# The second product of an MLP: its stationary operands moved by 16 bytes and read in steps of 1, 2 or 4 words

## The chip, the cores and the metric

The kernel runs on one core of one Trainium2 chip. The metric is the device time of one execution in microseconds (us), smaller is better. A core has five engines with queues of their own: TensorE (PE, matmuls; its weight loads are shown as PEld), VectorE (DVE), ScalarE (ACT), GpSimd (POOL) and SyncE (SP, which issues DMAs here).

## What is computed

Two layers, each of linear attention and an MLP, both with a layer norm in front and added to x. S = 2048 rows, D = 448, F = 1792, 16 heads of 28, all float32.

```python
def _B_ref(x, w1, b1, w2, b2):
    h = jnp.einsum("bsd,df->bsf", x, w1) + b1
    h = _gelu(h)
    return jnp.einsum("bsf,fd->bsd", h, w2) + b2
...
x = A_x
x = x + _A_ref(_layernorm(x, axis=-1), A_wqkv, A_wo)
x = x + _B_ref(_layernorm(x, axis=-1), B_w1, B_b1, B_w2, B_b2)
x = x + _A_ref(_layernorm(x, axis=-1), A_wqkv, A_wo)
x = x + _B_ref(_layernorm(x, axis=-1), B_w1, B_b1, B_w2, B_b2)
```

`_A_ref` is the linear attention: it forms q, k and v, applies phi to q and k, sums k times v over all rows, and divides.

## The kernel before

The 2048 rows are 16 tiles of 128 rows, and 4 tiles make a block. Every float32 product is made of three matmuls on operands in a shorter float format (F32R): each operand is split into a high part (the value rounded to F32R) and a low part (the remainder), and hi x hi, hi x lo and lo x hi are added up in the same PSUM bank.

A layer has a first phase (`phase1`) that runs over the 16 tiles and forms q, k and the sum over all rows, then a short stretch written out by hand as the string `ORDER`, then the MLP over four blocks. The layer's second half of attention for block b + 1 is worked in beside the MLP of block b, by the lists `PLAN_0`, `PLAN_1` and `PLAN`, whose tokens `behind` (lines 948 to 980) turns into calls. The order of all instructions is the order in which the program issues them; each engine works its queue from the front.

The MLP's loop is at lines 1029 to 1063. For each block it runs over i, the NF = 14 chunks of 128 of F. `mlp1` (lines 852 to 869) makes chunk i of the first product for the block's 512 rows: 11 matmuls at lines 858 to 862 with pieces of w1 as weights (the stationary operand, 128 x 128) and the block's x as the moving operand (512 columns), into `hp`. Then ACT applies gelu with the bias (line 864) to give `g`, ACT copies it to `gh` in F32R (line 867), and DVE subtracts to get `gl` (line 868). `gh` and `gl` have 128 partitions (the 128 rows of F of this chunk) and 512 words (the block's 512 rows of x, 128 for each tile j), in two buffers each, tags "A" and "B". `mlp2` (lines 871 to 898) is the second product: for each of the 4 tiles j it takes 128 columns of `gh` or `gl` as weights and a row of w2 (448 columns) as the moving operand, three matmuls at lines 891 to 893, accumulated over i in the PSUM bank `acc[j]`. In the very last chunk of the program the last tile is done in two halves of 224 columns (lines 883 to 885). After chunk 13 DVE adds the bank to x (line 896).

`mlp1` of chunk i + 1 is issued ahead of `mlp2` of chunk i, so that gelu, the copy and the subtraction of a chunk run beside the matmuls of the chunk before. The tags "A" and "B" also hold the split of x in the first phase (lines 442 and 443) and other tiles at lines 689, 776 and 777.

Two smaller places are touched. In layer 0, tiles 0 to 7 are transposed by PE, and the last 64 columns of a tile are copied twice over into a tile `tail` of 128 columns, two buffers (lines 411 to 413). And `b2b` (line 186) is a constant tile of 448 words that a DMA fills with b2 (line 1003), behind the first phase of layer 0; POOL adds it to x at line 820, in chunks 9 to 12 of each block.

Of the kernel before, what the change touches and what calls it, by code (L numbers as in the profile page):

```python
# [9 lines left out]
F32 = mybir.dt.float32  # L10
F32R = mybir.dt.float32r
# [11 lines left out]
def linear_attn_mlp_kernel(  # L23
# [12 lines left out]
    pe, act, dve, pool, sp = nc.tensor, nc.scalar, nc.vector, nc.gpsimd, nc.sync  # L36
# [15 lines left out]
    work = ctx.enter_context(tc.tile_pool(name="work", bufs=2))  # L52
# [9 lines left out]
    def bank(tag, bufs, name):  # L62
        return psum.tile([128, 512], F32, name=name, tag=tag, bufs=bufs)
# [4 lines left out]
        bufs = NH if tag == "H" else bufs  # L68
        return work.tile([128, D], dt, name=name, tag=tag, bufs=bufs)

    def t512(tag, bufs, name, dt=F32):
        return work.tile([128, 512], dt, name=name, tag=tag, bufs=bufs)

    def f(ap):
        return ap.bitcast(F32)
# [82 lines left out]

    ones = consts.tile([128, 128], F32R, name="ones")
    one = t512("e", 3, "one")[:, :128]  # L160
    dve.memset(one, 1.0)
    dve.tensor_copy(ones, one)
# [23 lines left out]
    b2b = consts.tile([128, D], F32, name="b2b")  # L186
# [5 lines left out]
    w2h = wts.tile([128, NF, D], F32R, name="w2h")  # L192
    w2l = wts.tile([128, NF, D], F32R, name="w2l")
# [23 lines left out]
    def ln_norm(stats, name):  # L217
        xs, mv, rs = stats
        xn = t512("xn", 2, name)
        dve.tensor_scalar(xn[:, :D], xs, mv[:, 0:1], rs, op0=OP.subtract, op1=OP.mult)  # L220
        return xn
# [69 lines left out]
    def turn(x, key, t):  # L291
        x = x[:, :D]
        if (key, t // 2) not in squares:
            squares[key, t // 2] = half("sq")
        sq = squares[key, t // 2].rearrange("p (m c u n) -> p c m u n", m=4, c=4, n=32)[:, :, :, t % 2]
        dve.transpose(sq[:, :3], x[:, :TL].rearrange("p (c m n) -> p c m n", c=3, n=32))
        dve.transpose(sq[:, 3].rearrange("p (u m) n -> p u m n", u=2),
                      x[:, TL:].rearrange("p (m n) -> p m n", n=32)[:, None].to_broadcast([128, 2, 2, 32]))
# [34 lines left out]
    def phi(o, name, into=None, tag="e"):  # L333

        e = t512(tag, 3 if tag == "e" else 2, name)[:, :D]
        act.activation(e, o, AF.Relu, scale=-1.0)
        act.activation(e, e, AF.Exp, scale=-1.0)
        into = e if into is None else into
        dve.scalar_tensor_tensor(into, o, 0.0, e, op0=OP.max, op1=OP.add)
        return into  # L340
# [60 lines left out]
    tails = {}  # L401
# [4 lines left out]
    def stage_n(l, t):  # L406

        xs, mv, rs = sts.pop((l, t))
        dve.tensor_scalar(xs, xs, mv[:, 0:1], rs, op0=OP.subtract, op1=OP.mult)
        xns[l, t] = xs  # L410
        if t < TURNED[l]:
            d = tails[l, t] = work.tile([128, 128], F32, name="tail", tag="tail", bufs=2)
            act.copy(d.rearrange("p (u n) -> p u n", u=2), xs[:, None, TL:].to_broadcast([128, 2, 64]))

    def stage_t(l, t):
# [191 lines left out]
    def phase1(l, tr):  # L607
# [6 lines left out]
        for t in range(l == 0, NT):  # L614
            norm = NORM[l][t] if t < len(NORM[l]) else ()
            for tok in STEPS.get((l, t), STEP).split():
                if tok[1:].isdigit() and tok[0] in "anv":
                    {"a": stage_a, "n": stage_n, "v": stage_t}[tok[0]](l, int(tok[1:]))
                elif tok == "q1":
                    stage_qphi(1)  # L620
# [9 lines left out]
                elif tok == "n":  # L630
                    for u in norm:
                        stage_n(l, u)
# [193 lines left out]
    def m_split(l, b, j):  # L826

        if j < 2:
            split_t(("m", l, b), j, *block(("m", l, b)).pieces(j), dve if j else pool)
        else:  # L830
            split_x(("m", l, b), j)
# [18 lines left out]
    gs = {}  # L850

    def mlp1(l, b, i):
        hp = bank("h", 2, "hp")
        s = slice(i * 128, (i + 1) * 128)
        x = blocks["m", l, b]
        o = hp.rearrange("p (t n) -> p t n", t=4)
        for c in range(3):
            pe.matmul(o, w1h[:, c, s], x.moving(x.hi, c), start=(c == 0), stop=False)  # L858
            pe.matmul(o, w1l[:, c, s], x.moving(x.hi, c), start=False, stop=False)  # L859
            pe.matmul(o, w1h[:, c, s], x.moving(x.lo, c), start=False, stop=False)  # L860
        pe.matmul(o, w1x[:, s], x.moving(x.hi, 3), start=False, stop=False)  # L861
        pe.matmul(o, w1x[:, s], x.moving(x.lo, 3), start=False, stop=True)  # L862
        g = t512("e", 3, "g")
        act.activation(g, hp, AF.Gelu_apprx_tanh, bias=b1s[:, i:i + 1])  # L864
        gh = t512("A", 2, "gh", F32R)
        gl = t512("B", 2, "gl", F32R)
        act.copy(gh, g)  # L867
        dve.tensor_sub(gl, g, f(gh))  # L868
        gs[i] = (gh, gl)

    def mlp2(l, b, i, acc):
        gh, gl = gs.pop(i)
        first, last = i == 0, i == NF - 1
        end = l == LAYERS - 1 and b == NB - 1
        for j in range(4):
            t = b * 4 + j
            s = slice(j * 128, (j + 1) * 128)
            if end and j == 3 and last:

                for h, eng in enumerate((act, sp)):  # L880
                    n = slice(h * D // 2, (h + 1) * D // 2)
                    o = bank("m", 2, "yh")[:, :D // 2]
                    pe.matmul(o, gh[:, s], w2h[:, i, n], start=True, stop=False)
                    pe.matmul(o, gh[:, s], w2l[:, i, n], start=False, stop=False)
                    pe.matmul(o, gl[:, s], w2h[:, i, n], start=False, stop=True)
                    xs = xt[l, t][:, n]
                    dve.tensor_tensor(xs, o, xs, op=OP.add)
                    eng.dma_start(x_d[l + 1][t * 128:(t + 1) * 128, n], xs)
                continue
            stop = last or (end and j == 3 and i == NF - 2)  # L890
            pe.matmul(acc[j], gh[:, s], w2h[:, i], start=first, stop=False)  # L891
            pe.matmul(acc[j], gh[:, s], w2l[:, i], start=False, stop=False)  # L892
            pe.matmul(acc[j], gl[:, s], w2h[:, i], start=False, stop=stop)  # L893
            if stop:
                xs = xt.pop((l, t)) if last else xt[l, t]
                dve.tensor_tensor(xs, acc[j], xs, op=OP.add)
                if last:
                    sp.dma_start(x_d[l + 1][t * 128:(t + 1) * 128, :], xs)
# [94 lines left out]
    for l in range(LAYERS):  # L993
        tr = SimpleNamespace(mp={})
        za, acc = phase1(l, tr)
# [9 lines left out]
        def pre(j):  # L1005
# [13 lines left out]
            x=lambda j: m_split(l, 0, j), tu=lambda j: turn(xns.pop(("m", l, j)), ("m", l, 0), j),  # L1019
            st=lambda j: store_sq(("m", l, 0), 0), sp=lambda j: spread(("m", l, 0), 0), pre=pre, b=biases)  # L1020
        for tok in ORDER.split():
            name, j = tok.rstrip("0123456789"), int("0" + tok.lstrip("abcdefghijklmnopqrstuvwxyzQTG"))
            getattr(tok_, name)(j)
        assert not fill and not qo
        table(AF.Gelu_apprx_tanh)
        q_z(l, 1, 0, tr)
        mlp1(l, 0, 0)
        trans_chunks(tr)
        for b in range(NB):
            acc = [bank("acc", 4, f"y{j}")[:, :D] for j in range(4)]  # L1030
# [5 lines left out]
            for i in range(NF):  # L1036
                if i + 1 < NF:
                    mlp1(l, b, i + 1)
                elif nxt:
                    mlp1(l, b + 1, 0)  # L1040
                if l == 0 and b == 0 and i:
                    background(1, 1)
                if i == NF - 2 and not nxt and l + 1 < LAYERS:
                    table(AF.Exp)
                if 9 <= i < 13:
                    add_bias(l, b, i - 9)
                if nxt:
                    behind(l, b, i, tr)
                elif l + 1 < LAYERS:
                    if i == 2:  # L1050
                        split_kq("k", st_k)
                    if i == 5:
                        split_kq("q", st_q)
                    if i in (3, 4, 6, 7, 8):
                        t = (3, 4, 6, 7, 8).index(i)
                        stage_a(l + 1, t)
                        stage_n(l + 1, t)
                        stage_t(l + 1, t)
                        if t % 2:
                            stage_sp(l + 1, t)  # L1060
                    if 9 <= i < 13:
                        stage_x(l + 1, i - 9)
                mlp2(l, b, i, acc)
# [28 lines left out]
```

## Time and profile before

| | |
|---|---|
| median of 2 runs | 877.35 us (877.15 to 877.54) |
| profiled execution, first to last instruction | 875.2 us |
| between that span and the median | 2.1 us |
| mean granted clock of TensorE | 0.999 |
| PE busy | 870.1 us, 99% |
| DVE busy | 491.2 us, 56% |
| ACT busy | 344.4 us, 39% |
| POOL busy | 221.1 us, 25% |

The profile is of one execution. A row of a group reads: line, engine, operation, what is written <- what is read, shapes, count | busy us, mean ns of one | idle time of the engine before it, with what ended most of it. In the timeline the columns are start and length in us, then engine and instruction. Matmuls are pipelined and their ends are modelled, so the length of a matmul is not what it costs in a stream; the distance of two starts is. PEld rows are the weight loads, which overlap matmuls. The blocks of the MLP of layer 0 start at about 143, 221, 299 and 377 us, those of layer 1 at about 573, 656, 734 and 812 us.

### The profile page before, as it was taken

To read this page: it belongs to the slowest core of one execution; us is meant where nothing else is said; L and a number is where in the kernel's file an instruction comes from. 1 tells how busy PE (TensorE), PEld (TensorE's weight loads), DVE (VectorE), ACT (ScalarE), POOL (GpSimd) and SP (SyncE) were. 2 spreads that over 40 slices of the span, in tenths; PEclk is the share of its full clock that TensorE was granted. 3 is DMA by queue.
4 is the path that set the end of the run, shared out by engine and by line. 5 is a ranking of instruction groups with operands and counts; after the bars stand their busy time and mean duration, and the time that the engine had idled before them with its cause. 6 is when DMAs were issued, how large, how long until landed. Compare 5 with 4: busy or idle time off the path is not lost.

```text
span 875.2 us, 11679 instructions
## 1 busy us (share of the span) xinstructions
PE 870.1 (99%) x4182; PEld 772.0 (88%) x4182; DVE 491.2 (56%) x958; ACT 344.4 (39%) x606; POOL 221.1 (25%) x250
## 2 busy tenths in 40 slices
PE   9999999999999999999999999999999999999998
PEld 8999988888888888888899998888888888888887
DVE  7878586658455443226477876864674483433112
ACT  6776635324323322333356665332233133223221
POOL 5566532235013112012222344110220140140000
PEclk9999999999999999999999999999999999999999
DMA  5474637633313402051145543352332423111001
GB/s 160 136 239 152 207 88 210 184 93 125 133 60 105 156 0 97 1 179 49 48 141 188 166 128 106 104 182 80 110 109 91 134 71 115 49 49 43 0 1 43
DMA packets 63642, 94.76 MB, mean 108 GB/s; under 512 B 8928, under 2 KB 58720, under 8 KB 63584
## 3 DMA queue, kind: packets, MB, share of 16 engines
q1 hardware_dynamic: 63408, 93.87, 33.5%
q8 instruction: 33, 0.54, 0.3%
q14 instruction: 25, 0.20, 0.1%
q10 hardware_dynamic: 176, 0.14, 0.0%
HBM read 56.17 MB, written 34.60 MB: 104 GB/s over the span
## 4 chain that ended last, share of the span: by engine, by line
PE 98%; DVE 0%; DMA 0%; POOL 0%; issue 0%; DVEq 0%; POOLq 0%
PE y L893 10%; PE y L892 10%; PE y L891 10%; PE hp L859 9%; PE hp L860 9%; PE hp L858 9%; PE hp L861 3%; PE hp L862 3%; PE psk L326 2%; PE psq L325 2%; PE psq L327 2%; PE psq L326 2%; PE psk L327 2%; PE psk L325 2%; PE G L534 2%; PE G L535 2%
## 5 line engine op out<-in xcount | busy, mean ns | idle before, releaser
L868 DVE TENSOR_TENSOR gl<-g,gh 128x512 fp32r<-128x512 f32 x112 | 82.6, 737 | 300.0 <-ACT gh L867 300.0
L864 ACT ACTIVATE g<-hp,b1s 128x512 f32<-128x512 f32 x112 | 77.1, 688 | 406.6 <-PE hp L862 401.8
L893 PE MATMUL y<-w2h,gl 128*128 128x448 f32 x447 | 163.3, 365 | 0.0
L892 PE MATMUL y<-w2l,gh 128*128 128x448 f32 x447 | 163.3, 365 | 0.0
L891 PE MATMUL y<-w2h,gh 128*128 128x448 f32 x447 | 163.3, 365 | 0.0
L859 PE MATMUL hp<-XH,w1l 128*128 128x512 f32 x336 | 131.5, 392 | 0.0
L858 PE MATMUL hp<-XH,w1h 128*128 128x512 f32 x336 | 131.2, 391 | 0.0
L860 PE MATMUL hp<-XL,w1h 128*128 128x512 f32 x336 | 131.2, 391 | 0.0
L214 POOL TENSOR_TENSOR brs<-bve,mhalf 128x1 f32<-128x1 f32 x64 | 39.4, 616 | 283.9 <-DVE bve L212 280.8
L891 PEld LDWEIGHTS y<-w2h,gh 128*128 128x128 f32 x447 | 84.0, 188 | 9.0
L892 PEld LDWEIGHTS y<-w2l,gh 128*128 128x128 f32 x447 | 84.0, 188 | 8.3
L893 PEld LDWEIGHTS y<-w2h,gl 128*128 128x128 f32 x447 | 84.0, 188 | 6.6
L860 PEld LDWEIGHTS hp<-XL,w1h 128*128 128x128 f32 x336 | 63.1, 188 | 14.1 <-issue 0.6
L859 PEld LDWEIGHTS hp<-XH,w1l 128*128 128x128 f32 x336 | 63.1, 188 | 11.3
L858 PEld LDWEIGHTS hp<-XH,w1h 128*128 128x128 f32 x336 | 63.1, 188 | 10.8
L867 ACT CAST gh<-g 128x512 fp32r<-128x512 f32 x112 | 69.7, 622 | 3.6
L751 POOL TENSOR_TENSOR pz<-pq,zb 128x448 f32<-128x448 f32 x32 | 36.6, 1147 | 82.6 <-DVE dn L757 65.9
L445 POOL TENSOR_TENSOR xnl<-x,xnh 128x384 fp32r<-128x384 f32 x32 | 35.0, 1092 | 72.6 <-ACT xnh L444 40.6
L315 DVE TENSOR_TENSOR XL<-sp,XH 128x512 fp32r<-128x512 f32 x50 | 44.4, 893 | 4.1 <-ACT XH L314 4.1
L862 PE MATMUL hp<-XL,w1x 128*128 128x512 f32 x112 | 43.6, 389 | 0.0
L861 PE MATMUL hp<-XH,w1x 128*128 128x512 f32 x112 | 43.6, 389 | 0.0
L820 POOL TENSOR_TENSOR x<-x,b2b 128x448 f32<-128x448 f32 x32 | 42.0, 1332 | 0.0
(169 smaller groups left out, 1566.8 us busy)
## 6 DMA issues: line engine op xcount, KB each, us to landing
x<-in_A_x_dram SPq DMA_DIRECT2D x32, 224.0 KB, 3.9
pq_d<-eq SPq DMA_DIRECT2D x32, 224.0 KB, 2.8
pq<-pq_d SPq DMA_DIRECT2D x32, 224.0 KB, 3.2
sq_m<-sq SPq DMA_DIRECT2D x14, 512.0 KB, 2.8
sp<-sq_m SPq DMA_DIRECT2D x56, 128.0 KB, 2.9
x<-x_d SPq DMA_DIRECT2D x32, 224.0 KB, 3.2
sq_a<-sq SPq DMA_DIRECT2D x12, 512.0 KB, 2.9
sp<-sq_a SPq DMA_DIRECT2D x48, 128.0 KB, 2.9
```

The source lines that it names most:

```text
L315: eng.tensor_tensor(lo.rearrange("p (c i n) -> p c i n", c=4, n=32), x, f(h), op=OP.subtract)
L858: pe.matmul(o, w1h[:, c, s], x.moving(x.hi, c), start=(c == 0), stop=False)
L859: pe.matmul(o, w1l[:, c, s], x.moving(x.hi, c), start=False, stop=False)
L860: pe.matmul(o, w1h[:, c, s], x.moving(x.lo, c), start=False, stop=False)
L861: pe.matmul(o, w1x[:, s], x.moving(x.hi, 3), start=False, stop=False)
L862: pe.matmul(o, w1x[:, s], x.moving(x.lo, 3), start=False, stop=True)
L864: act.activation(g, hp, AF.Gelu_apprx_tanh, bias=b1s[:, i:i + 1])
L867: act.copy(gh, g)
L868: dve.tensor_sub(gl, g, f(gh))
L891: pe.matmul(acc[j], gh[:, s], w2h[:, i], start=first, stop=False)
L892: pe.matmul(acc[j], gh[:, s], w2l[:, i], start=False, stop=False)
L893: pe.matmul(acc[j], gl[:, s], w2h[:, i], start=False, stop=stop)
```

## The change

`gh` and `gl` get tiles of 576 words, and a chunk's 512 words begin at an offset that depends on the chunk: `gh` at `at(i)`, `gl` at `at(i + 7)`. Most blocks take `i % 16 * 4` words, that is 16 bytes more from chunk to chunk. Inside the 512 words, the columns of the four tiles j are interleaved by a step of 1, 2 or 4 words, which the table `DEALT` gives by layer and block: with 1 they stand as before, each tile's 128 words on end; with 2, two tiles share 256 words, every other word each; with 4, all four share the 512 words, every fourth word each. ACT and DVE write `gh` and `gl` in that order, and PE reads its weights in that step.

| layer, block | step in words | offset of chunk i in words |
|---|---|---|
| 0, 0 | 1 | 4 (i mod 16) |
| 0, 1 | 2 | 4 (i mod 16) |
| 0, 2 | 4 | 4 (i mod 16) |
| 0, 3 | 1 | 8 (i mod 8) |
| 1, 0 | 2 | 4 (i mod 16) |
| 1, 1 | 1 | 4 (i mod 16) |
| 1, 2 | 1 | 4 ((i + 2) mod 16) |
| 1, 3 | 1 | 0 |

All other tiles with the tags "A" and "B" keep offset 0. `tail` has no tile of its own any more; it takes one of two halves of `b2b` in turn.

```diff
-    def t512(tag, bufs, name, dt=F32):
-        return work.tile([128, 512], dt, name=name, tag=tag, bufs=bufs)
+    def t512(tag, bufs, name, dt=F32, at=0):
+        n = 576 if tag in "AB" else 512
+        return work.tile([128, n], dt, name=name, tag=tag, bufs=bufs)[:, at:at + 512]
...
-            d = tails[l, t] = work.tile([128, 128], F32, name="tail", tag="tail", bufs=2)
+            d = tails[l, t] = b2b[:, t % 2 * 128:][:, :128]
             act.copy(d.rearrange("p (u n) -> p u n", u=2), xs[:, None, TL:].to_broadcast([128, 2, 64]))
...
-        gh = t512("A", 2, "gh", F32R)
-        gl = t512("B", 2, "gl", F32R)
-        act.copy(gh, g)
-        dve.tensor_sub(gl, g, f(gh))
-        gs[i] = (gh, gl)
+        step, at = DEALT[l][b]
+        gh = t512("A", 2, "gh", F32R, at(i))
+        gl = t512("B", 2, "gl", F32R, at(i + 7))
+
+        def dealt(x):
+            return x.rearrange("p (h n u) -> p h u n", h=4 // step, u=step)
+
+        g4 = g.rearrange("p (h u n) -> p h u n", h=4 // step, u=step)
+        act.copy(dealt(gh), g4)
+        dve.tensor_sub(dealt(gl), g4, f(dealt(gh)))
+        gs[i] = [dealt(x) for x in (gh, gl)]
+
+    DEALT = (
+        ((1, lambda i: i % 16 * 4), (2, lambda i: i % 16 * 4), (4, lambda i: i % 16 * 4), (1, lambda i: i % 8 * 8)),
+        ((2, lambda i: i % 16 * 4), (1, lambda i: i % 16 * 4), (1, lambda i: (i + 2) % 16 * 4), (1, lambda i: 0)),
+    )
...
-            s = slice(j * 128, (j + 1) * 128)
+            s = (slice(None), j // step, j % step)
...
-            pe.matmul(acc[j], gh[:, s], w2h[:, i], start=first, stop=False)
-            pe.matmul(acc[j], gh[:, s], w2l[:, i], start=False, stop=False)
-            pe.matmul(acc[j], gl[:, s], w2h[:, i], start=False, stop=stop)
+            pe.matmul(acc[j], gh[s], w2h[:, i], start=first, stop=False)
+            pe.matmul(acc[j], gh[s], w2l[:, i], start=False, stop=False)
+            pe.matmul(acc[j], gl[s], w2h[:, i], start=False, stop=stop)
```

The two halves of the last tile (lines 883 to 885) change in the same way.

More of the change, by code (lines that the diff above doesn't have):

```diff
@@ L864, in mlp1 @@
         act.activation(g, hp, AF.Gelu_apprx_tanh, bias=b1s[:, i:i + 1])
-        gh = t512("A", 2, "gh", F32R)
-        gl = t512("B", 2, "gl", F32R)
-        act.copy(gh, g)
-        dve.tensor_sub(gl, g, f(gh))
-        gs[i] = (gh, gl)
+        step, at = DEALT[l][b]
[11 more added lines that the diff above has]
+    )
     def mlp2(l, b, i, acc):
         gh, gl = gs.pop(i)
+        step = DEALT[l][b][0]
         first, last = i == 0, i == NF - 1
@@ L882, in mlp2 @@
                     o = bank("m", 2, "yh")[:, :D // 2]
-                    pe.matmul(o, gh[:, s], w2h[:, i, n], start=True, stop=False)
-                    pe.matmul(o, gh[:, s], w2l[:, i, n], start=False, stop=False)
-                    pe.matmul(o, gl[:, s], w2h[:, i, n], start=False, stop=True)
+                    pe.matmul(o, gh[s], w2h[:, i, n], start=True, stop=False)
+                    pe.matmul(o, gh[s], w2l[:, i, n], start=False, stop=False)
+                    pe.matmul(o, gl[s], w2h[:, i, n], start=False, stop=True)
                     xs = xt[l, t][:, n]
```

## Prediction

> **What bounds the kernel now.** I read the head of the page first, then the waits of PE, then the costliest groups with their shapes kept apart, and last the timeline of one chunk of the MLP.
>
> ```profile
> span 875.2 us, 11679 instructions
> PE 870.1 (99%) x4182; PEld 772.0 (88%) x4182; DVE 491.2 (56%) x958; ACT 344.4 (39%) x606; POOL 221.1 (25%) x250
> PEclk9999999999999999999999999999999999999999
> PE 98%; DVE 0%; DMA 0%; POOL 0%; issue 0%; DVEq 0%; POOLq 0%
> ```
>
> PE has work for the whole span, at a full clock, and 98% of the chain that ended last is PE itself. The waits of PE hold nothing of the MLP:
>
> ```profile
> engine line waited for: us in total, times, longest us
> PE warm L167 <- DVE one L161: 1.1, 1, 1.1
> PE tp L264 <- ACT tail L413: 0.2, 1, 0.2
> ```
>
> So the time changes only where the change makes PE's own instructions longer or shorter, or makes PE wait for gh or gl. What it touches on PE are the three lines of the second product:
>
> ```profile
> L893 PE MATMUL y<-w2h,gl 128*128 128x448 f32 x447 | 163.3, 365 | 0.0
> L892 PE MATMUL y<-w2l,gh 128*128 128x448 f32 x447 | 163.3, 365 | 0.0
> L891 PE MATMUL y<-w2h,gh 128*128 128x448 f32 x447 | 163.3, 365 | 0.0
> ...
> L326 PE MATMUL psq<-wq,XH 128*128 128x448 f32 x96 | 35.1, 366 | 0.0
> ...
> L535 PE MATMUL G<-kl,xnh 128*128 128x448 f32 x90 | 32.9, 365 | 0.0
> ...
> L891 PEld LDWEIGHTS y<-w2h,gh 128*128 128x128 f32 x447 | 84.0, 188 | 9.0
> ```
>
> 3 x 447 = 1341 matmuls. The 365 ns are a modelled length and overlap with the next one's; what counts is start to start. One chunk of layer 0, block 2, in the timeline (start, length, engine):
>
> ```profile
> 299.35 0.36 PE L891 MATMUL y<-w2h,gh 128*128 128x448 f32 x1
> 299.36 0.19 PEld L892 LDWEIGHTS y<-w2l,gh 128*128 128x128 f32 x1
> 299.55 0.37 PE L892 MATMUL y<-w2l,gh 128*128 128x448 f32 x1
> ...
> 301.58 0.37 PE L893 MATMUL y<-w2h,gl 128*128 128x448 f32 x1
> 301.79 0.39 PE L858 MATMUL hp<-XH,w1h 128*128 128x512 f32 x1
> ...
> 304.07 0.39 PE L862 MATMUL hp<-XL,w1x 128*128 128x512 f32 x1
> 304.07 0.19 PEld L891 LDWEIGHTS y<-w2h,gh 128*128 128x128 f32 x1
> 304.29 0.36 PE L891 MATMUL y<-w2h,gh 128*128 128x448 f32 x1
> ```
>
> The 12 matmuls of the second product start from 299.35 to 301.58: 11 gaps, 2.23 us, **203 ns** each. The 11 of the first product start from 301.79 to 304.07: 10 gaps, **228 ns** each. The 64 columns more cost 25 ns, 0.39 ns a column; 448 columns would be 177 ns by that, and 26 ns stand beside them. Each weight load starts within 0.01 us of the start of the matmul before its own. Whether it or the stream of columns sets the 203 ns is seen at the end of the kernel, where only 224 columns stream:
>
> ```profile
> 870.83 0.19 PEld L884 LDWEIGHTS yh<-w2l,gh 128*128 128x128 f32 x1
> 870.93 0.27 PE L884 MATMUL yh<-w2l,gh 128*128 128x224 f32 x1
> 870.94 0.19 PEld L885 LDWEIGHTS yh<-w2h,gl 128*128 128x128 f32 x1
> 871.05 0.27 PE L885 MATMUL yh<-w2h,gl 128*128 128x224 f32 x1
> ...
> 871.38 0.27 PE L885 MATMUL yh<-w2h,gl 128*128 128x224 f32 x1
> ```
>
> With half the columns, and the same weights, the gap falls to (871.38 - 870.93) / 4 = **113 ns**, and a matmul starts 0.10 to 0.11 us after its load started, though the load's row says 0.19 (its tail overlaps). So a contiguous load of 128 columns needs at most 113 ns between matmuls, and the 448 columns hide it with 203 - 113 = 90 ns to spare. That margin decides this case.
>
> **The change part by part.**
>
> *Places 16 bytes further (all blocks but layer 1, block 3).* No instruction is added. A load of 512 bytes a partition begins elsewhere. At worst it touches one more piece of memory, and 90 ns of margin lie over it: I take 0. From below: if the 26 ns beside the columns came from where the weights lie against w2, up to 26 ns could be won in 1341 - 168 = 1173 matmuls (12 x 14 = 168 stay in the block without an offset), 30 us. But psq and G, with other tiles in other places, have the same 366 and 365 ns, so I take no gain and keep that end for a rival. With the margin gone, the offset would cost what the longer load does, below.
>
> *Steps of 2 words (layer 0 block 1 and layer 1 block 0: 336 matmuls).* A load now reaches over 128 x 8 = 1024 bytes a partition instead of 512. The trace shows no load in steps. Ends: 113 ns, if only elements count (hidden), and 2 x 113 = 226 ns, if bytes passed over count at the load's own contiguous rate. The nearest row of a faster reader is the first product's moving operand: 512 x 4 = 2048 bytes a partition in 228 ns, so PE's reading of 1024 bytes fits in 114 ns. I take 114: hidden, cost 0.
>
> *Steps of 4 words (layer 0 block 2: 168 matmuls).* A load reaches over 128 x 16 = 2048 bytes. Ends: 113 ns (hidden, 0) and 4 x 113 = 452 ns. The nearest row is again 2048 bytes of moving operand in 228 ns; twice the load's own 105 ns plus the 10 ns until it starts is 220 ns. I take **220 ns**, which is over the 203: the load ends last, and each gap grows by 17 ns. In a chunk 11 of the 12 loads stand behind a matmul of 448 columns; the first stands behind one of 512, whose 228 ns still hide it. So 14 x 11 = 154 gaps x 17 ns = **2.6 us**.
>
> [...]
>
> *Writing gh and gl in steps (ACT L867, DVE L868).* Same instructions and elements, other places. The chain of one chunk, and of the tightest chunk in a block with steps (layer 1, block 0, chunk 0):
>
> ```profile
> 300.27 0.62 ACT L867 CAST gh<-g 128x512 fp32r<-128x512 f32 x1
> 300.93 0.69 DVE L868 TENSOR_TENSOR gl<-g,gh 128x512 fp32r<-128x512 f32 x1 [2.12 <-ACT gh L867]
> 304.50 0.19 PEld L893 LDWEIGHTS y<-w2h,gl 128*128 128x128 f32 x1
> ...
> 572.01 0.69 DVE L868 TENSOR_TENSOR gl<-g,gh 128x512 fp32r<-128x512 f32 x1 [2.18 <-ACT gh L867]
> 573.14 0.19 PEld L893 LDWEIGHTS y<-w2h,gl 128*128 128x128 f32 x1
> ```
>
> gl is ready at 301.62 and first loaded at 304.50: 2.88 us. Ends: nothing, or both instructions doubled, 0.62 + 0.69 = 1.31 us, still hidden. At 572.70 the reserve is 0.44 us: doubled, PE would wait 0.87 us, once. Behind a longer gl on DVE stand the next block's steps, and DVE is busy only 28.3 of 78 us there (windows):
>
> ```profile
> core 0: us, PE busy (x) PEld busy (x) DVE busy (x) ACT busy (x) POOL busy (x), PEclk, DMA share, GB/s
> 299.00:377.00 78.00, 78.00 (x367) 68.64 (x366) 28.32 (x54) 22.70 (x36) 7.69 (x8) 1.00 0.15 51
> ```
> ```profile
> L315 DVE TENSOR_TENSOR XL<-sp,XH 128x512 fp32r<-128x512 f32 x4 | 2.7, 683 | 0.0
> ```
>
> L315, which reads and writes in another order in runs of 32 words, takes 683 ns beside 691 for gl; that is the nearest row, so I take 0.
>
> *Tail in halves of b2b, larger A and B.* Two halves taken in turn stand where two buffers stood; the eight copies and their transposes are over long before b2b is loaded:
>
> ```profile
> L413 ACT COPY tail<-x x8: 289/298/299, 6.6 to 41.1; 128x128 f32<-128x128 f32 x8
> L257 PE MATMUL tp<-ident,tail x6: 272/272/273, 17.8 to 51.4; 128*128 128x128 f32 x6
> L1003 SPq DMA_DIRECT2D b2b<-in_B_b_dram x1: 1588/1588/1588, 112.3 to 112.3; - x1
> ```
>
> The load on SP's queue gains a wait for the last transpose (51.4 us), 61 us before it is issued; nothing queued behind it moves. If the halves were held as one tile, a copy (0.30 us) could wait for one transpose: at most 8 x 0.3 = 2.4 us; I take 0.
>
> *Sum.* The profiled span is 875.2 us, the median of the runs 877.35, so 2.1 us lie outside it. 875.2 + 0 + 0 + 2.6 + 0 + 0 + 2.1 = 879.9, **880.0 us**.
>
> **The rivals.**
>
> *A. The steps are hidden too.* If the load counts elements alone, it stays at 113 ns under 203, and the time is 877.4. For it: 90 ns of margin. Against it: no row shows a stepped read.
>
> *B. The load takes its reads from the stream.* The 26 ns beside the columns would be the load's reads, and grow with the bytes it reaches over. That is +26 ns in 336 matmuls (8.7 us) and +78 ns in 168 (13.1 us): 21.8 us, 899. With half of the 26 ns, 10.9 us, 888; I put it at 890. For it: 26 ns is much for a mere change of weights. Against it: the trace shows no pair of matmuls without a load to compare. [...]
>
> *C. The load passes over bytes at its own rate.* 226 ns for steps of 2, 452 ns for steps of 4. Then 28 x 11 = 308 gaps x 23 ns = 7.1 us, and in block 2 of layer 0 154 x (452 - 203) = 38.3 us and 14 x (452 - 228) = 3.1 us: 48.5 us, 925.9, slower by 5.5%. It decides by itself, with steps of 4 alone, from a load of x ns with 154 (x - 203) + 14 (x - 228) = 17.5 us, which is 2%: x = 309 ns. For it: 113 ns is the only rate of loading that the trace shows. Against it: PE's other operand passes the same bytes in 228.
>
> *D. Faster.* The 26 ns come from a clash of places and fall away in 1173 matmuls: down to 847; half of it 862. Against it: equal times for all tiles of 448 columns.
>
> *E. A late gl.* The writes double and the tail waits: 880.0 + 0.9 + 2.4 = 883.3.
>
> **How the numbers follow.** My forecast 0.34; A 0.24; B 0.16; C 0.15; E 0.06; D 0.05. The likeliest alone, with a load of 210 to 230 ns, adds 1.1 to 4.2 us: 878.4 to 881.5. For the range I leave out C and D, 0.20 together: from 876.0, just under A, to 899.0, the upper end of B. About 2% is what a measurement of this kernel can tell from no change; that is 859.8 to 894.9. Over it lie C and the upper quarter of B, 0.19; under it most of D, 0.04; within it 0.77.
>
> **What would show it.** In the timeline of layer 0, block 2, second product: 220 ns from start to start (203: A; 240 to 280: B; 300 and more: C), with the load rows there longer than 188 ns. In the blocks with steps of 2: 203 (A and mine), 216 or more (B, C). In blocks with offsets alone 203; less would be D. L867 and L868 by block show what writing in steps costs, and the waits of PE must stay without L891 and L893. I am wrong if the blocks with offsets alone differ from layer 1, block 3, or if the sum of blocks 1 and 2 doesn't give the difference of the spans.

## The result, and the profile after

The changed kernel takes 884.26 us (883.89 to 884.64, 2 runs) against 877.35 us (877.15 to 877.54, 2 runs): 1.0075 times as long, 95% interval 1.0046 to 1.0104. That is 6.9 us more; the forecast was 2.7 us more, in a range of 876.0 to 899.0. The direction is as forecast, the size two and a half times as large. The profiled execution has a span of 882.2 us, 7.0 us more than before. The page's head, its chain, and the costliest groups that changed (lines 904 to 906 are the old 891 to 893, line 874 the old 867, line 875 the old 868):

```profile
span 882.2 us, 11679 instructions
PE 875.9 (99%) x4182; PEld 781.5 (89%) x4182; DVE 496.7 (56%) x958; ACT 351.5 (40%) x606; POOL 221.3 (25%) x250
PE 98%; DMA 1%; DVE 0%; ACT 0%; POOL 0%; issue 0%; SPq 0%; DVEq 0%; ACTq 0%
L875 DVE TENSOR_TENSOR gl<-g,gh 128x512 fp32r<-128x512 f32 x112 | 88.0, 786 | 303.0 <-ACT gh L874 299.2
L906 PE MATMUL y<-w2h,gl 128*128 128x448 f32 x447 | 165.1, 369 | 0.0
L906 PEld LDWEIGHTS y<-w2h,gl 128*128 128x128 f32 x447 | 92.8, 208 | 5.3
L874 ACT CAST gh<-g 128x512 fp32r<-128x512 f32 x112 | 77.7, 694 | 3.6
```

PE is still 98% of the chain, and its waits still hold nothing of the MLP:

```profile
engine line waited for: us in total, times, longest us
PE warm L168 <- DVE one L162: 1.1, 1, 1.1
PE tp L265 <- DVE x L410: 0.7, 1, 0.7
PE tp L265 <- ACT b2b L414: 0.7, 1, 0.7
```

So PE's own instructions became longer. The mean over 447 weight loads of L906, 208 ns instead of 188, hides where. Block by block, the distance from one block's first matmul of the second product to the next block's tells it (starts taken from the trace; the fourth column reaches over the first phase of layer 1, the last one from the first such matmul of layer 1, block 3 to the last):

```
us               start   0,0    0,1    0,2    0,3     1,0    1,1    1,2    1,3
before          143.11  78.12  78.12  78.12  195.47  78.12  78.12  78.12  63.33
after           143.35  78.24  78.48  83.44  195.82  78.42  78.21  78.28  63.33
difference       +0.24  +0.12  +0.36  +5.32   +0.35  +0.30  +0.09  +0.16   0.00
```

They add up to 6.9 us. Of it 5.3 us lie in the one block with steps of 4, 0.7 us in the two blocks with steps of 2, 0.7 us in the four with offsets alone, and 0.2 us in the start. The timeline of the block with steps of 4, to be laid beside the chunk that the prediction shows:

```profile
299.85 0.40 PE L863 MATMUL hp<-XL,w1x 128*128 128x512 f32 x1
300.08 0.37 PE L904 MATMUL y<-w2h,gh 128*128 128x448 f32 x1
300.29 0.40 PE L905 MATMUL y<-w2l,gh 128*128 128x448 f32 x1
300.30 0.33 PEld L906 LDWEIGHTS y<-w2h,gl 128*128 128x128 f32 x1
300.52 0.39 PE L906 MATMUL y<-w2h,gl 128*128 128x448 f32 x1
300.53 0.33 PEld L904 LDWEIGHTS y<-w2h,gh 128*128 128x128 f32 x1
300.75 0.40 PE L904 MATMUL y<-w2h,gh 128*128 128x448 f32 x1
...
302.64 0.40 PE L906 MATMUL y<-w2h,gl 128*128 128x448 f32 x1
302.65 0.21 PEld L859 LDWEIGHTS hp<-XH,w1h 128*128 128x128 f32 x1
302.87 0.39 PE L859 MATMUL hp<-XH,w1h 128*128 128x512 f32 x1
```

The load is 0.33 us long instead of 0.19, and from 300.29 to 302.64 ten gaps take 2.35 us: **235 ns** from start to start, where 203 stood and 220 was forecast. The first gap is 210 ns, and the gap behind the 512 columns of L863 is 230 ns, as before. The gap from the last of the twelve to the first product (302.64 to 302.87) has some 235 ns again, though the load in it is a contiguous one. So eleven gaps of a chunk grow, as counted in the prediction, but in the records each stands one place later than its load; the run on the price of a load shows why.

### The profile page after: what moved, and what is told of

Read it like the earlier page. It is cut to its first block, busy times and chain, and to the rows that moved or that the text cites. A ratio compares the mean times of both kernels' runs of the same rounds, so it can differ in the third digit from the quotient of the medians.

```text
span 882.2 us, 11679 instructions
## 1 busy us (share of the span) xinstructions
PE 875.9 (99%) x4182; PEld 781.5 (89%) x4182; DVE 496.7 (56%) x958; ACT 351.5 (40%) x606; POOL 221.3 (25%) x250
## 4 chain that ended last, share of the span: by engine, by line
PE 98%; DMA 1%; DVE 0%; ACT 0%; POOL 0%; issue 0%; SPq 0%; DVEq 0%; ACTq 0%
PE y L905 10%; PE y L906 10%; PE y L904 10%; PE hp L860 9%; PE hp L861 9%; PE hp L859 9%; PE hp L863 3%; PE hp L862 3%; PE psk L327 2%; PE psq L326 2%; PE psq L327 2%; PE psq L328 2%; PE psk L328 2%; PE psk L326 2%; PE G L537 2%; PE G L535 2%
## 5 line engine op out<-in xcount | busy, mean ns | idle before, releaser
L875 DVE TENSOR_TENSOR gl<-g,gh 128x512 fp32r<-128x512 f32 x112 | 88.0, 786 | 303.0 <-ACT gh L874 299.2
L905 PE MATMUL y<-w2l,gh 128*128 128x448 f32 x447 | 165.2, 370 | 0.0
L906 PE MATMUL y<-w2h,gl 128*128 128x448 f32 x447 | 165.1, 369 | 0.0
L904 PEld LDWEIGHTS y<-w2h,gh 128*128 128x128 f32 x447 | 92.5, 207 | 7.7
L905 PEld LDWEIGHTS y<-w2l,gh 128*128 128x128 f32 x447 | 92.6, 207 | 7.2
L906 PEld LDWEIGHTS y<-w2h,gl 128*128 128x128 f32 x447 | 92.8, 208 | 5.3
L874 ACT CAST gh<-g 128x512 fp32r<-128x512 f32 x112 | 77.7, 694 | 3.6
L863 PE MATMUL hp<-XL,w1x 128*128 128x512 f32 x112 | 43.9, 392 | 0.0
```

Of the source, the lines that this page charges most:

```text
L874: act.copy(dealt(gh), g4)
L875: dve.tensor_sub(dealt(gl), g4, f(dealt(gh)))
L904: pe.matmul(acc[j], gh[s], w2h[:, i], start=first, stop=False)
L905: pe.matmul(acc[j], gh[s], w2l[:, i], start=False, stop=False)
L906: pe.matmul(acc[j], gl[s], w2h[:, i], start=False, stop=stop)
```

## The experiments

Theory 1: a weight load in steps takes longer and, where it outlasts the columns that stream meanwhile, ends last; the offsets act separately, by where weights and moving operand stand to each other. The rivals: B of the prediction, the load takes reads from the stream, so that a step adds the same at every width; that steps of 2 cost by themselves and offsets nothing; that the slower writes hold PE up.

**Steps alone.** All offsets of the changed kernel are 0.

```diff
-        ((1, lambda i: i % 16 * 4), (2, lambda i: i % 16 * 4), (4, lambda i: i % 16 * 4), (1, lambda i: i % 8 * 8)),
-        ((2, lambda i: i % 16 * 4), (1, lambda i: i % 16 * 4), (1, lambda i: (i + 2) % 16 * 4), (1, lambda i: 0)),
+        ((1, lambda i: 0), (2, lambda i: 0), (4, lambda i: 0), (1, lambda i: 0)),
+        ((2, lambda i: 0), (1, lambda i: 0), (1, lambda i: 0), (1, lambda i: 0)),
```

> The changed kernel with every offset set to 0; the steps of 1, 2 and 4 words stay. Theory 1 (the stepped load ends last; the offsets act for themselves by where weights and moving operand stand to each other): layer 0 block 2 keeps its 83.4 us (78.1 before), the blocks with steps of 2 and of 1 go back to 78.1 us, 12 matmuls of the second product to 2.433 us; span 880.4 to 880.8. Rival (steps of 2 cost by themselves, offsets nothing): the two blocks with steps of 2 keep 78.4 to 78.5, the others are at 78.1; span 881.1.

Measured: 883.74 us, ratio 1.0074 (1.0059 to 1.0089), span 881.3. By blocks, in the manner of the table: 78.12, 78.47, 83.86, 195.59, 78.46, 78.12, 78.12, 63.33. The rival is right for steps of 2: they cost 0.35 us a block with no offset at all, half of it in the second product (12 matmuls 2.444 us instead of 2.433) and half in the first product between them (229.4 ns a matmul instead of 228.3). Theory 1 had them free. The blocks with steps of 1 are at 78.12 as both said. The block with steps of 4 costs 5.7 us, so the offsets took 0.4 us off it.

**Offsets alone.** All steps of the changed kernel are 1.

```diff
+        ((1, lambda i: i % 16 * 4), (1, lambda i: i % 16 * 4), (1, lambda i: i % 16 * 4), (1, lambda i: i % 8 * 8)),
+        ((1, lambda i: i % 16 * 4), (1, lambda i: i % 16 * 4), (1, lambda i: (i + 2) % 16 * 4), (1, lambda i: 0)),
```

> The changed kernel with every step set to 1; the offsets stay. Theory 1: layer 0 block 2 falls from 83.4 us to 78.2, the blocks with offsets keep 0.1 to 0.35 us over 78.1, since the time of 12 matmuls depends on the place (2.400 to 2.460 us); span 876.0 to 876.8. Rival (steps cost, offsets nothing): all blocks at 78.1 us, 2.433 us for each 12; span 875.4.

Measured: 878.51 us, ratio 1.0013 (1.0003 to 1.0023), span 877.1. By blocks: 78.24, 78.20, 78.20, 195.80, 78.24, 78.21, 78.28, 63.33: 0.1 us over before, as theory 1 has it. The 12 matmuls of a chunk take 2.40 to 2.46 us, and a chunk's time comes again, to within 0.02 us, wherever its offsets come again (chunk 0, offsets of 0 and 112 bytes: 2.400 in all five blocks that have it; chunk 8: 2.441 in two of them and 2.461 in three). The span is higher than expected by 0.3 us because the second product started at 144.04 us; that start lies between 142.4 and 145.2 us in the profiles of this case, and the changed kernel's own +0.24 lies well within it.

**The price of a load.** The second product is not computed: it takes its weights from the block's high part of x, in steps of 1 to 16 words, and streams fewer columns in most blocks. All offsets are 0.

```diff
+    WIDE = ((448, 224, 112, 336), (448, 224, 112, 336))
+    STEPS_OF = (1, 1, 2, 2, 3, 3, 4, 4, 6, 6, 8, 8, 16, 16)
...
-            pe.matmul(acc[j], gh[s], w2h[:, i], start=first, stop=False)
+            n, u = WIDE[l][b], STEPS_OF[i]
+            w = blocks["m", l, b].hi[:, :128 * u].rearrange("p (n u) -> p u n", u=u)[:, j % u]
+            pe.matmul(acc[j][:, :n], w, w2h[:, i, :n], start=first, stop=False)
```

(The two other matmuls change alike.)

> Measures the price of a weight load: the second product takes all its weights from the block's high part of x (2048 words a partition) in steps of 1, 2, 3, 4, 6, 8 and 16 words, two chunks each, and streams 448, 224, 112 or 336 columns by block; so the second product is not computed, the rest of its columns are left out, and gh and gl are made but not used. Theory 1 (the load ends last): the gap is the larger of the stream's (203 at 448 columns, about 158 at 336, 113 and less below) and the load's own, which is the same at every width: 113 ns for 1, 235 for 4. Within it, by pieces of memory touched: 235 also for 6, 8 and 16; by bytes passed over: 470 at 8 and 940 at 16. Rival B (the load takes its reads from the stream): the step adds the same 33 ns at every width, so a step of 4 gives about 146 ns at 224 columns and about 190 at 336.

Measured: 881.0 us once, span 879.3; what counts here is each chunk by itself. Two rows of 224 columns with steps of 1, 224 columns with steps of 4, and 112 columns with steps of 4, from its timeline:

```profile
229.80 0.28 PE L910 MATMUL y<-w2l,XH 128*128 128x224 f32 x1
229.91 0.27 PE L911 MATMUL y<-w2h,XH 128*128 128x224 f32 x1
...
260.31 0.40 PE L910 MATMUL y<-w2l,XH 128*128 128x224 f32 x1
260.43 0.33 PEld L911 LDWEIGHTS y<-w2h,XH 128*128 128x128 f32 x1
260.55 0.40 PE L911 MATMUL y<-w2h,XH 128*128 128x224 f32 x1
...
336.07 0.40 PE L910 MATMUL y<-w2l,XH 128*128 128x112 f32 x1
336.23 0.33 PEld L911 LDWEIGHTS y<-w2h,XH 128*128 128x128 f32 x1
336.30 0.40 PE L911 MATMUL y<-w2h,XH 128*128 128x112 f32 x1
```

0.11, 0.24 and 0.23 us from start to start. The means of ten gaps in each chunk (without the first), from the trace, in ns:

```
step in words   bytes passed   112 columns   224   336   448
 1                  512            112        112   154   203
 2                 1024            118        119   153   203
 3                 1536            175        175   176   205
 4                 2048            234        233   233   233
 6                 3072            225        226   229   230
 8                 4096            239        242   244   245
16                 8192            219        224   225   227
```

Each entry is the larger of two numbers: the stream's, at the right and above, and the load's, which is the same, to within 8 ns, down to 112 columns. Rival B would have 146 ns for steps of 4 at 224 columns; it has 233, so B falls. The load's price stops rising at steps of 4 words, which are 16 bytes: bytes passed over (470 and 940 ns for 8 and 16, rival C's rate) are not what counts, and theory 1 with pieces of memory has 235 for all of them, where 219 to 245 stand. Counted in pieces of 16 bytes, the step at which the price stops rising in this table, steps of 2, 3 and 4 touch 64, 96 and 128 pieces, and 118, 175 and 233 ns are 1.84, 1.82 and 1.82 ns a piece; above 4 words each of the 128 columns has its own piece. The contiguous load, 32 pieces, takes 112 ns at 112 and at 224 columns, not the 58 ns of that count; against it steps of 3 take 1.6 times as long and steps of 4 take 2.1 times. A step of 4 has 233 or 234 ns at every width; beside it the first product's matmuls grow from 228.3 to 231.0 ns, in the run with steps alone.

The gaps at both ends of a chunk, which the table leaves out, say what a recorded start is. One chunk with 112 columns and steps of 1:

```profile
301.03 0.21 PE L909 MATMUL y<-w2h,XH 128*128 128x112 f32 x1
301.08 0.28 PE L910 MATMUL y<-w2l,XH 128*128 128x112 f32 x1
301.19 0.28 PE L911 MATMUL y<-w2h,XH 128*128 128x112 f32 x1
...
302.20 0.27 PE L911 MATMUL y<-w2h,XH 128*128 128x112 f32 x1
302.31 0.45 PE L859 MATMUL hp<-XH,w1h 128*128 128x512 f32 x1
302.61 0.40 PE L860 MATMUL hp<-XH,w1l 128*128 128x512 f32 x1
```

The first gap, whose load had the 512 columns ahead to hide behind, is 0.05 us, and the first of the first product, behind a load that had only 112 columns, is 0.30 us instead of 0.23. So what a load outlasts is recorded behind the start of its own matmul, one gap later. The first gap is then the stream alone: 50, 100, 150 and 199 ns at 112, 224, 336 and 448 columns with steps of 1, which is 0.45 ns a column with nothing beside (512 columns by that: 228 ns, as the first product has). With steps of 4 it is 52 to 54, 106 and 157 ns at 112, 224 and 336 columns: 2 to 7 ns more, where a load of 233 ns outlasts the 228 ahead by 5.

**A map of places.** All steps 1; offsets from a table of pairs, in units of 16 bytes.

```diff
-        step, at = DEALT[l][b]
-        gh = t512("A", 2, "gh", F32R, at(i))
-        gl = t512("B", 2, "gl", F32R, at(i + 7))
+        step, (p, q) = 1, PLACES[l][b](i)
+        gh = t512("A", 2, "gh", F32R, p % 16 * 4)
+        gl = t512("B", 2, "gl", F32R, q % 16 * 4)
...
+    PLACES = (
+        (lambda i: (i, 0), lambda i: (0, i), lambda i: (i, i), lambda i: (i, i + 8)),
+        (lambda i: (i + 2, 0), lambda i: (0, i + 2), lambda i: (i, i + 7), lambda i: (0, 7)),
+    )
```

> All steps 1; the offsets of gh and gl, in units of 16 bytes, go through (i,0), (0,i), (i,i), (i,i+8), (i+2,0), (0,i+2), (i,i+7) and (0,7) over the eight blocks. Theory 1 (place against the moving operand decides): the time of 12 matmuls is a function of the two offsets modulo 16 alone: (0,0) gives 2.433 us in every block, (0,7) 2.400 in all 14 chunks of the last block, and (2,9) 2.455 as in the changed kernel. Rival (it depends on the order of the chunks, not on the places): the first chunks of each block differ from its later ones whatever the offset.

Measured: 877.62 us once, span 875.9. The pairs give 2.400 to 2.481 us for 12 matmuls: (0,0) 2.433 in the three blocks that have it, (0,5) 2.481 in two, (0,1) and (0,13) 2.400, and (0,7) 2.400 in the 13 chunks of the last block that have twelve whole matmuls. So place decides and not the order of the chunks. Theory 1 is short in two things. The same pair differs by up to 0.017 us from block to block ((0,7) has 2.414 in one chunk), where other matmuls stand between the chunks, so what runs ahead seems to count a little too. And that the place counts against the moving operand is not shown, since w2 never moved.

**Write apart from read.** All offsets 0; layer 0 writes in steps of 4 and reads contiguous weights, layer 1 the other way round.

```diff
-        step, at = DEALT[l][b]
+        (step, reads), at = DEALT[l][b]
...
+        step = reads
         gs[i] = [dealt(x) for x in (gh, gl)]
```

> All offsets 0. Layer 0 writes gh and gl in steps of 4 words and reads them as contiguous weights; layer 1 writes them contiguous and reads them in steps of 4, so the rows of the second product are mixed up in both. Theory 1 (only the stepped load costs): the MLP of layer 0 keeps 12 matmuls at 2.433 us though the copy to gh takes 1.12 us and gl 1.10 us (2.3 us and more of reserve hide them); that of layer 1 has 2.80 to 2.82 us for 12 with the copy at 0.62 us. Span: 875.2 + 56 x 0.38 = 896.5. Rival (the slower writes hold PE up): layer 0 has some of the loss, with L904 and L906 in the waits of PE.

Measured: 903.06 us once, span 901.3. The groups of layer 0's MLP and then of layer 1's:

```profile
L875 DVE TENSOR_TENSOR gl<-g,gh 128x512 fp32r<-128x512 f32 x56 | 63.4, 1132 | 118.7 <-ACT gh L874 118.6
L874 ACT CAST gh<-g 128x512 fp32r<-128x512 f32 x55 | 61.4, 1117 | 1.7
L907 PEld LDWEIGHTS y<-w2h,gl 128*128 128x128 f32 x222 | 41.7, 188 | 4.3 <-DVE gl L875 1.1
```
```profile
L907 PEld LDWEIGHTS y<-w2h,gl 128*128 128x128 f32 x222 | 74.4, 335 | 0.0
L874 ACT CAST gh<-g 128x512 fp32r<-128x512 f32 x55 | 34.2, 621 | 1.8
```

Writing in steps of 4 costs ACT 1117 ns instead of 622 and makes no load longer; reading in steps of 4 makes the loads 335 ns and no write longer. Layer 0 has 2.43 us for 12 matmuls in 54 of its 56 chunks. The rival holds in the two that have least reserve (0.43 and 0.37 us in the kernel before): chunk 0 of block 0 takes 2.829 and chunk 13 of block 3 takes 2.909, where gl comes late, 0.9 us together. The blocks of layer 1 cost 5.7 us each. The span is 4.8 us over what was expected, for the most part by three things: 2.1 us by a later start (145.18 us), 0.9 us by the late gl, and 0.4 us a block in the first product (231.0 ns a matmul instead of 228.3 beside steps of 4, a number of the run with steps alone).

**gl alone 112 bytes further.** The kernel before, with the best pair of the map in every chunk.

```diff
-    def t512(tag, bufs, name, dt=F32):
-        return work.tile([128, 512], dt, name=name, tag=tag, bufs=bufs)
+    def t512(tag, bufs, name, dt=F32, at=0):
+        n = 576 if tag == "B" else 512
+        return work.tile([128, n], dt, name=name, tag=tag, bufs=bufs)[:, at:at + 512]
...
-        gl = t512("B", 2, "gl", F32R)
+        gl = t512("B", 2, "gl", F32R, 28)
```

(And the tail in halves of b2b.)

> The kernel before with one thing changed: gl stands 112 bytes further (7 x 16), gh where it was, all steps 1 (and the tail in halves of b2b, to make room). Theory 1 (place decides, and the survey's pair (0,7) holds): 2.400 us for each 12 matmuls in all 112 chunks instead of 2.433, so 112 x 0.033 = 3.7 us less: 873.5, span 871.5. Rival (the survey's gain was that of one block): 877.

Measured: 872.15 us, ratio 0.9941 (0.9927 to 0.9955), span 870.4. One chunk of layer 0, block 2:

```profile
298.37 0.36 PE L892 MATMUL y<-w2h,gh 128*128 128x448 f32 x1
298.57 0.37 PE L893 MATMUL y<-w2l,gh 128*128 128x448 f32 x1
298.78 0.36 PE L894 MATMUL y<-w2h,gl 128*128 128x448 f32 x1
298.97 0.36 PE L892 MATMUL y<-w2h,gh 128*128 128x448 f32 x1
...
300.58 0.36 PE L894 MATMUL y<-w2h,gl 128*128 128x448 f32 x1
300.77 0.39 PE L859 MATMUL hp<-XH,w1h 128*128 128x512 f32 x1
```

From 298.37 to 300.77 stand 12 gaps in 2.40 us, 200 ns each instead of 203; in 24 of the 112 chunks it is 2.414 us, so the second product gains 3.3 us. The gain of the whole is 5.0 us instead of 3.7: the first product, whose tiles were not touched, falls from 228.3 to 226.7 ns a matmul as well, 1.8 us in all. That this is the offset and not a new layout of the other tiles is seen in the map of places, where all blocks have one layout: there the first product has 226.7 ns in the block with (0,7) alone, and 227.9 or more in the seven others.

**More places.** As the last one, with xnl and XL moved too, XL of the MLP's blocks by another amount in each block.

```diff
-            self.lo = work.tile([128, 2048], F32R, name="XL", tag="XL", bufs=2)
+            at = 28 if key[0] == "a" else 4 * ((0, 1, 7, 13), (4, 8, 9, 15))[key[1]][key[2]]
+            self.lo = work.tile([128, 2112], F32R, name="XL", tag="XL", bufs=2)[:, at:at + 2048]
...
-        lo = t512("B", 2, "xnl", F32R)
+        lo = t512("B", 2, "xnl", F32R, 28)
```

> As the kernel with gl 112 bytes further, and the low part of the first phase's x, xnl, as well as XL of the attention's blocks stand 112 bytes further too; XL of the MLP's blocks stands 0, 16, 112, 208, 64, 128, 144 and 240 bytes further, block by block. Theory 1 (any pair of weights and moving operand obeys the same rule): the products of the first phase, with the same order hi, hi, lo of weights, fall from 203 to 200 ns from start to start, some 1000 matmuls, 3 us; the first product falls in some blocks from 228 to at best 227 ns, and grows in others. Rival (the rule is that of gh, gl and w2 alone): the first phase stays at 203 and 228 does not move.

Measured: 876.59 us once, span 874.9. The first product obeys places too, but every move made it longer: 227.4 ns a matmul in the block with XL where it was, 229.1 to 231.9 in the others (blocks of 77.6 us, and of 77.8 to 78.6). The second product, which does not read XL, changed with it in some blocks: 2.453 us for 12 matmuls, where 2.400 to 2.415 stood, in six of the 14 chunks of layer 0, block 1. The projections (the three matmuls of a piece) fell by 0.57 us in all and the sum over rows by 0.6 us, some 40% of what was expected; the pair of matmuls at the end of each projection stayed at 203 and 204 ns.

**The tail alone.** The kernel before, with the tail in halves of b2b.

```diff
-            d = tails[l, t] = work.tile([128, 128], F32, name="tail", tag="tail", bufs=2)
+            d = tails[l, t] = b2b[:, t % 2 * 128:][:, :128]
```

> The kernel before with the tail in halves of b2b and nothing else changed. My forecast of that step is 0: 877.2 to 877.5, and the start of the second product at 143.1 give or take 0.7 us, which is how far it stood apart in the runs so far. Rival (the tail in b2b waits): 0.3 to 2.4 us more.

Measured: 877.19 us against 877.16, ratio 1.0000 (0.9992 to 1.0009), with the second product's start at 143.62 us. The step costs nothing, as forecast.

**The first phase too.** As the one with gl alone, with xnl and the attention's XL moved by 112 bytes and the MLP's XL where it was.

```diff
+            at = 28 if key[0] == "a" else 0
```

> The kernel with gl 112 bytes further, and xnl and the XL of the attention's blocks 112 bytes further too; the MLP's XL stays where it was, since every other place of it made the first product longer (block times 77.6 to 78.6 us against 77.5). By the rows of the survey with the MLP's XL moved, the first phase's projections fall by 0.57 us and the sum over rows by 0.6 us: 1.1 us under the 872.2 of the kernel with gl alone, 871.0. Rival (the places in the first phase gain nothing as a whole): 872.2.

Measured: 870.84 us, ratio 0.9929 (0.9916 to 0.9943), span 869.1. It is the fastest version of this study, 6.8 us under the kernel before. Against the one with gl alone (0.9941) the intervals overlap, so the 1.1 us are likely but not shown as a whole. In the traces the stretch that holds the first phase of layer 1 falls from 194.85 to 194.51 us; the second product of layer 0 starts 1.0 us earlier, but that start differs by more between profiles anyway.

## Why the prediction was right, and where its size was off

*The whole:* 884.26 us lies in the range, but above the 878.4 to 881.5 that the forecast gave for itself alone. Rival E's 883.3 stands nearer, but by chance: PE has no wait for gl after the change, and the tail alone costs nothing. The two signs of being wrong came, both in small: the blocks with offsets alone differ from layer 1, block 3, by their 0.1 to 0.2 us, and blocks 1 and 2 of layer 0 give 5.7 of the 7.0 us.

*What bounds the kernel:* right. PE has no wait in the MLP after the change, and 6.7 of the 6.9 us are in PE's own gaps; the rest is the start.

*Steps of 4 words:* the mechanism was right, the size off by half. The forecast took 220 ns for the load, from twice its contiguous time, and 154 gaps x 17 ns = 2.6 us. The load takes 235 ns, 2.1 times, so it is 154 x 32 ns = 4.9 us. The first load of a chunk, which the forecast held hidden behind 512 columns, is only nearly so: the first gap is 216 ns instead of 201, which makes it 5.2 us in the second product; with the first product it is 5.3 us in the block. Of the two rows that were weighed, 2048 bytes of moving operand in 228 ns was the nearer one (32 x 154 against 25 x 154 = 3.9 us), and the lower one was taken. A margin makes this term steep: the time counts only above 203 ns, so 15 ns in the load were nearly the whole term again.

*Steps of 2 words:* forecast 114 ns and hidden. The load alone needs 118 ns, so it is hidden with 85 ns to spare, but 1 ns on each matmul of both products comes on top, 0.35 us a block, 0.7 us in all. Its cause was not found; the load's own time can't be it.

*Places:* forecast 0, measured +0.1 to +0.2 us a block and +0.35 us for the stretch that holds layer 0, block 3 and the next first phase (195.59 of its 195.82 us stand in the run with the tail alone as well, so 0.23 of it is the offsets'), at most 0.7 us in all. The reason given, that psq and G have the same time with tiles in other places, was a weak one: the map shows 2.400 to 2.481 us by place, and no row of before showed that those tiles differ in place in the sense that counts. So D had a true core: 33 ns a chunk can be won, 0.6% of the kernel with gl alone and the first product's share, and the change did not win it because its offsets run through good and bad places alike. The 30 us of its end rest on a reading that was wrong: 26 ns beside the columns, from the difference of 203 and 228 ns. By the first gaps of the load run 448 columns stream in 199 ns and nothing stands beside them, so of the 203 ns only about 3 were there to be won. (The block without an offset has 165 matmuls of 448 columns, not 168; that changes nothing.)

*Writes in steps:* the cost of 0 was right, the reason was not. The row taken as nearest, L315, had no loss, but with steps of 4 the writers do: ACT takes 1126 ns for gh instead of 622, and DVE a median of 1104 for gl instead of 691 (its subtraction reads gh in the same steps). With steps of 2 ACT takes 658 ns and DVE a median of 693; the mean of 734 below holds one long instruction of 1261 ns, and the kernel before has one of 1266 in the same block. The reserve of 2.9 us hides all of it. The groups of the 14 chunks of the one block and of the other:

```profile
L874 ACT CAST gh<-g 128x512 fp32r<-128x512 f32 x14 | 15.8, 1126 | 0.4
L875 DVE TENSOR_TENSOR gl<-g,gh 128x512 fp32r<-128x512 f32 x14 | 15.6, 1117 | 49.7 <-ACT gh L874 49.7
```
```profile
L875 DVE TENSOR_TENSOR gl<-g,gh 128x512 fp32r<-128x512 f32 x14 | 10.3, 734 | 31.5 <-ACT gh L874 31.5
L874 ACT CAST gh<-g 128x512 fp32r<-128x512 f32 x14 | 9.2, 658 | 0.4
```

The tight chunk, layer 1, block 0, chunk 0, is harmless here, where it has steps of 2. With steps of 4 it was not run; the chunk of layer 0 in the same place, with the same reserve, cost 0.4 us in the run that writes in steps of 4, half of the bound.

*Tail:* right, 0.

*Rivals:* A falls by the 235 ns, B by the table of widths (and by steps of 2, where it had 216 ns or more), C by the 118 and 233 ns of steps of 2 and 4, where it had 226 and 452, and by steps of 8 and 16, E by the waits of PE.

## What to carry to other kernels

In these runs a weight load was hidden only while it was shorter than the matmul ahead of it: against the 203 ns of 448 columns, 118 ns at steps of 2 words was, and 233 ns at steps of 4 was not. Measure both at few columns, and estimate a new reading pattern by the pieces of 16 bytes that it touches: from the table, 1.82 to 1.84 ns a piece at steps of 2, 3 and 4 words, and 112 ns for the contiguous load of 128 float32 columns, the least that was measured. Before an average over a kernel is believed, cut it into the blocks that differ: 208 ns as the mean load was 188, 195 and 331 in the blocks with steps of 1, 2 and 4.

## What was not expected of the hardware

- The place of the weights, moved by 0 to 240 bytes, changes the distance of two matmuls from 200 to 207 ns (12 matmuls: 2.400 to 2.481 us), the same to within 0.02 us a chunk at each return of the pair of offsets. Why is open; that the reads of weights and moving operand meet in the same part of the memory was not tested.
- A better place in one product sped up the other, which was not touched, from 228.3 to 226.7 ns a matmul.
- A load in steps of 16 words (219 to 227 ns) is shorter than one in steps of 8 (239 to 245) or 4 (233).
- A step of 4 words costs the writers nearly as much as the reader, whose load grows 2.1 times: ACT's copy of 512 words takes 1126 ns instead of 622 (658 at steps of 2 words), and DVE's subtraction 1104 instead of 691 (693 at steps of 2 words).
- A matmul's recorded start stands ahead of the wait for its own weights: with 112 columns the first gap of a chunk is 50 ns, and the time that a load outlasts the stream shows one gap later.
